# Where the fallback program lies in the instruction streams: behind each engine's first instructions, jumped over with a prefetch hint

## The chip, the cores and the metric

One core of one Trainium2 chip. Times are device microseconds of an execution. Runs carry a state, fast or slow; ratios use fast runs alone. The experiments ran on several chips, each beside `before` in the same rounds, and are compared with that. The profile is one execution; its span runs from the core's first to its last instruction and is about 1.8 us shorter than the time.

## The reference

Multi-head attention over one sequence of 2048 tokens, width 448, 16 heads of 28, in bf16:

```python
qkv = (x @ wqkv).reshape(B, S, 3, H, Dh).transpose(2, 0, 3, 1, 4)
q, k, v = qkv[0], qkv[1], qkv[2]
scores = einsum("bhqd,bhkd->bhqk", q, k) * Dh ** -0.5
o = einsum("bhqk,bhkd->bhqd", softmax(scores), v)
return o.transpose(0, 2, 1, 3).reshape(B, S, D) @ wo
```

## The kernel before

It holds two programs. The fast one (`F`) takes the softmax without its maximum and counts at the end whether every row sum lay in a safe range. The flag says yes for these inputs. If it said no, a slower general program (`R`) would run. Every engine gets both as one stream: fast program, flag, branch, general program, end.

```python
def body(e, eng):
    F.emit_engine(e, eng, fs)                     # the fast program, this engine's part
    eng.wait_ge(fs["dve"], F.flag_op.count)
    ok = eng.value_load(F.flag_ap)
    with eng.If(ok == 0):                         # not taken here: jumped over
        ...                                       # barrier
        R.emit_engine(e, eng, rs)                 # the general program
        ...
    if e == "sp":
        for gr in F.finish:                       # the output transfers have landed
            eng.wait_ge(gr.sem, 16 * gr.n)
```

As built, the general program has 6865 instructions on PE, 1161 on ACT, 595 on DVE, 107 on POOL and 45 on SP.

The fast program opens like this. ACT issues the loads of the first weights. SP issues four transposing loads of x, a quarter each. PE runs 14 groups of four matmuls on zeros: they start 0.40 to 0.43 us apart up to 4.55 us and 0.22 us apart from 4.84 us on, so that PE is in its short step when the first weights and the first quarter of x are there. Then PE projects K and Q of the first quarter, DVE copies K and ACT copies Q (`QT`) out of PSUM. PE then wants the second quarter of x, multiplies the first scores, and ACT begins its 362 exponentials, which are its bound to the end (87% of the chain that ended last).

## Time and profile before

| | before |
|---|---|
| time, median of fast runs | 355.51 us (355.34 to 355.72) |
| span of the profile | 353.3 us |
| weights and first quarter of x landed | 6.26 and 5.89 us |
| second quarter of x landed | 8.77 us |
| first exponential starts | 9.58 us |
| flag computed | 348.43 us |
| flag to end of the span | 4.90 us |

Read it as four stretches: an opening to 9.58 us, bound by loads (DMA share 0.99; PE's projections start 0.09 us after the weights have landed); 333 us of exponentials; 5.8 us of last products and copies up to the flag; and a close of 4.90 us after it, in which no engine computes. The lines behind it are in the prediction.

### The profile page before, as it was taken

Reading aid. Unit: us, or ns where it says so; the run is one execution under the profiler, and the core shown is the slowest. Engines: PE = TensorE matmul, PEld = TensorE weight load, DVE = VectorE, ACT = ScalarE, POOL = GpSimd, SP = SyncE. Lnnn points to the kernel's source line nnn. Section 1 sums busy time; section 2 is a strip of 40 time slices with the busy share of each in tenths; the row PEclk is TensorE's granted clock in tenths of the full one; section 3 lists DMA queues with packets and bytes.
Section 4 is the critical chain, followed back from the end, with each engine's and each line's share of the span. In section 5 each row is a group of like instructions: output and inputs, shape, how many; then the busy total and the mean of one; then the engine's idle time right before and its main releaser. Section 6 shows DMA issues by size and latency. Waiting matters only on the chain.

```text
span 353.3 us, 8533 instructions
## 1 busy us (share of the span) xinstructions
PE 332.5 (94%) x3601; PEld 97.5 (28%) x3601; DVE 328.9 (93%) x557; ACT 335.5 (95%) x367; POOL 68.4 (19%) x157
## 2 busy tenths in 40 slices
PE   7999999999999999999999999999999899999993
PEld 3333232223322222332322222223222222222231
DVE  1788999999999999999999999999999999999962
ACT  2999999999999999999999999999999999999971
POOL 7332030042043013104030121340120301010010
PEclk9999999999999999999999999999999999999999
DMA  9910010010100000010100101010000101020111
GB/s 186 216 24 2 15 39 2 5 32 2 32 19 18 0 5 32 0 34 3 33 2 4 33 1 33 3 33 2 13 21 5 32 30 58 16 71 13 42 34 59
DMA packets 21604, 10.63 MB, mean 30 GB/s; under 512 B 15676, under 2 KB 19516, under 8 KB 21560
## 3 DMA queue, kind: packets, MB, share of 16 engines
q1 hardware_dynamic: 20136, 9.71, 11.4%
q8 instruction: 30, 0.49, 0.6%
q10 hardware_dynamic: 1424, 0.31, 0.5%
q14 instruction: 14, 0.11, 0.1%
HBM read 5.83 MB, written 2.08 MB: 22 GB/s over the span
## 4 chain that ended last, share of the span: by engine, by line
ACT 87%; PE 7%; DVE 2%; DMA 2%; SPq 0%; issue 0%
ACT PT L935 87%; PE ps L846 3%; PE ps L894 2%; DMA xT<-in_x_dram 2%; DVE PD L961 1%; PE ps L758 1%; DVE PD L955 1%; DVE PD L963 1%; SPq L442 0%; PE ps L533 0%; PE ps L804 0%; PE ps L793 0%; PE ps L681 0%; PE ps L780 0%; DVE OUTS L810 0%
## 5 line engine op out<-in xcount | busy, mean ns | idle before, releaser
L935 ACT ACTIVATE PT<-ps 128x1024 bf16<-128x1024 f32 x362 | 332.4, 1252 | 1.3 <-PE ps L894 1.3
L955 DVE TENSOR_SCALAR PD<-ps 128x512 int16<-128x512 f32 x300 | 192.7, 682 | 7.8 <-PE ps L894 6.7
L894 PE MATMUL ps<-QT,KT 28*128 28x512 bf16 x1024 | 148.9, 384 | 11.1 <-ACT PT L935 9.5
L846 PE MATMUL ps<-PD,VC 128*32 128x512 f16 x900 | 80.0, 386 | 0.9 <-DVE PD L963 0.5
L894 PEld LDWEIGHTS ps<-QT,KT 28*128 28x128 bf16 x1024 | 37.9, 91 | 149.7 <-ACT PT L935 141.4
L846 PE MATMUL ps<-PT,V 128*32 128x512 bf16 x724 | 64.5, 385 | 0.7 <-DVE KT L517 0.2
L730 POOL TENSOR_TENSOR QT<-RB,OTS 128x128 bf16<-128x128 f32 x60 | 30.8, 544 | 161.7 <-DMA RB<-scr_r 161.5
L963 DVE TENSOR_SCALAR PD<-PD 128x2048 int16<-128x2048 int16 x75 | 53.5, 713 | 0.0
L961 DVE TENSOR_SCALAR PD<-PD 128x2048 int16<-128x2048 int16 x75 | 53.2, 709 | 0.1
L533 PE MATMUL ps<-xT,w_raw 128*32 128x512 bf16 x512 | 42.6, 385 | 1.4 <-DMA xT<-in_x_dram 0.6
L568 POOL TENSOR_SCALAR V<-VX 128x224 bf16<-128x224 f32 x32 | 12.6, 412 | 113.0 <-DVE VX L517 112.9
L846 PEld LDWEIGHTS ps<-PD,VC 128*32 128x32 bf16 x900 | 19.1, 94 | 32.6 <-issue 22.2
L846 PEld LDWEIGHTS ps<-PT,V 128*32 128x32 bf16 x724 | 15.7, 94 | 23.9 <-issue 20.7
L555 PE MATMUL ps<-w_raw,xT 128*128 128x112 bf16 x256 | 20.8, 215 | 0.0
L574 POOL TENSOR_SCALAR VC<-VX 128x112 bf16<-128x112 f32 (+1 forms) x48 | 19.0, 408 | 1.0
L555 PEld LDWEIGHTS ps<-w_raw,xT 128*128 128x128 bf16 x256 | 13.3, 98 | 10.9 <-issue 9.5
L533 PEld LDWEIGHTS ps<-xT,w_raw 128*32 128x32 bf16 x512 | 10.0, 94 | 19.5 <-issue 13.1
L681 PE MATMUL ps<-wop,QT 128*128 128x448 bf16 x48 | 13.5, 358 | 0.1
L517 DVE CAST KT<-ps 128x512 bf16<-128x512 f32 x16 | 11.0, 686 | 0.4 <-PE ps L533 0.3
L515 DVE TENSOR_SCALAR QT<-ps 128x512 bf16<-128x512 f32 x15 | 10.3, 685 | 0.3 <-PE ps L533 0.2
L713 DVE COPY OTS<-ps 128x512 f32<-128x512 f32 x15 | 10.3, 684 | 0.0
L517 DVE COPY VX<-ps 128x448 f32<-128x448 f32 x16 | 9.9, 618 | 0.3 <-PE ps L555 0.2
(50 smaller groups left out, 50.5 us busy)
## 6 DMA issues: line engine op xcount, KB each, us to landing
RB<-scr_r SPq DMA_DIRECT2D x60, 64.0 KB, 2.0
out_dram<-OUTS SPq DMA_DIRECT2D x16, 112.0 KB, 1.7
w_raw<-in_wqkv_dram SPq DMA_DIRECT2D x3, 249.0 KB, 4.3
wop<-in_wo_dram SPq DMA_DIRECT2D x16, 24.5 KB
w_raw<-in_wqkv_dram ACTq DMA_DIRECT2D x3, 87.0 KB, 3.9
scr_l<-OTS SPq DMA_DIRECT2D x15, 8.0 KB
LT<-scr_l SPq DMA_DIRECT2D x15, 8.0 KB, 1.6
scr_r<-RS SPq DMA_DIRECT2D x15, 8.0 KB, 1.4
```

The source lines that it names most:

```text
L517: fe = (lambda e: e.tensor_copy(evac[0](), evac[1](hold[0].banks[0])))
L533: ins = e.matmul(ps[32 * h:32 * h + 32, b * 512:(b + 1) * 512], w_raw[:, wi(c, it), col:col + 32], xT[:, it, c * 512:(c + 1) * 512], start ...
L555: ins = e.matmul(ps[:, b * 512 + j * GD:b * 512 + (j + 1) * GD], xT[:, it, n * 128:(n + 1) * 128], w_raw[:, wi(c, it), 2 * D + g * GD:2 * ...
L574: sc = P.add("pool", (lambda e, dst=dst, j=j: e.tensor_scalar(dst, src, TERM_C[j], 1.0, ALU.mult, ALU.mult)), deps=[ev, ms_c1[j]], after=[ ...
L681: return e.matmul(bank(hold[0].banks[0])[:, 0:D], QT[:, gg, n * 128:(n + 1) * 128], wop[:, gg, :], start=(gg == 0), stop=(gg == G - 1))
L730: nm = P.add("pool", (lambda e, k=k: e.tensor_tensor(QT[:, g, c * QCH + k * w_:c * QCH + (k + 1) * w_], RB[:, ub, k * w_:(k + 1) * w_], OT ...
L846: return e.matmul(ps[32 * h:32 * h + 32, accb(u) * 512:(accb(u) + 1) * 512], lhsT, rhs, start=first, stop=False, skip_group_check=True, ti ...
L894: return e.matmul(bank(b), KT[32 * h:32 * h + DH, g, kt * 128:(kt + 1) * 128], QT[32 * h:32 * h + DH, g, c * QCH:(c + 1) * QCH], start=Tru ...
L935: ex = P.add("act", (lambda e, p0=p0, w=w, b0=b0: e.activation(PT[:, p0 * 512:(p0 + w) * 512], bank(b0, w), AF.Exp, scale=ESCALE)), deps=[ ...
L955: r = P.add("dve", (lambda e, hold=hold, zs=zs, h=h: e.tensor_scalar(PD[:, zs, 0, h * 512:(h + 1) * 512], bank(hold[0].banks[0]), ZBIAS, 0 ...
L961: h1 = P.add("dve", (lambda e, zs=zs: e.tensor_scalar(PD[:, zs, 1, :], PD[:, zs, 0, :], float(TERM_D[1]), None, ALU.add)), deps=rs_ + [z_l ...
L963: h2 = P.add("dve", (lambda e, zs=zs: e.tensor_scalar(PD[:, zs, 2, :], PD[:, zs, 0, :], float(TERM_D[2]), None, ALU.add)), deps=rs_ + [z_l ...
```

## The change

Its intent is to take the far jump out of the close. The general program moves to a place behind the first few instructions of each engine. A jump there passes it by, and a prefetch hint (the engine's first instruction) is to have the target fetched by then. The main program falls through to its end.

```diff
+HEAD_OPS = {"sp": 3, "act": 6, "dve": 1, "pool": 13, "pe": 6}
 def body(e, eng):
-    F.emit_engine(e, eng, fs)
-    eng.wait_ge(fs["dve"], F.flag_op.count)
-    ok = eng.value_load(F.flag_ap)
-    with eng.If(ok == 0):
+    hint = eng.mark_branch_hint_location()
+    F.emit_engine(e, eng, fs, 0, lead, waited)          # lead = HEAD_OPS[e]
+    eng.br(go).branch_hint(hint)
+    with nc.body(slow, valid_engines=[eng.engine]):
         ...                                             # the general program, as it was
+        eng.br(end)
+    with nc.body(go, valid_engines=[eng.engine]):
+        F.emit_engine(e, eng, fs, lead, None, waited)
+        eng.wait_ge(fs["dve"], F.flag_op.count)
+        ok = eng.value_load(F.flag_ap)
+        eng.br_eq(ok, 0, on_true=slow, on_false=end)
+    nc.switch_bb(end)
```

## The prediction

> **What bounds the kernel now.** The change touches no arithmetic, so I first ask which part of the span could feel it. I read the page's busy line and chain, then the table of stretches, then the records of the closing instructions line by line, then the opening.

> ```profile
> PE 332.5 (94%) x3601; PEld 97.5 (28%) x3601; DVE 328.9 (93%) x557; ACT 335.5 (95%) x367; POOL 68.4 (19%) x157
> ACT PT L935 87%; PE ps L846 3%; PE ps L894 2%; DMA xT<-in_x_dram 2%; DVE PD L961 1%; PE ps L758 1%; DVE PD L955 1%; DVE PD L963 1%; SPq L442 0%; PE ps L533 0%; PE ps L804 0%; PE ps L793 0%; PE ps L681 0%; PE ps L780 0%; DVE OUTS L810 0%
> ```

> For 87% of the span the chain is ScalarE's exponentials. The diff leaves those instructions and their order alone, so the body should keep its length; only what comes before the first exponential and after the last output copy can move. The table of stretches (start:end, length, then busy time of PE, weight loads, DVE, ACT, POOL) sizes them:

> ```profile
> 0.00:9.60 9.60, 7.62 (x97) 2.95 (x97) 1.61 (x4) 2.10 (x4) 6.52 (x17) 1.00 0.99 194
> 9.60:342.70 333.10, 319.75 (x3452) 91.61 (x3451) 323.75 (x541) 332.35 (x362) 60.17 (x136) 1.00 0.10 25
> 348.40:353.40 5.00, 0.00 (x0) 0.00 (x0) 0.03 (x1) 0.00 (x0) 0.00 (x0) 0.95 0.27 88
> ```

> The last row is the find: for 5.0 us no engine computes, and the span still runs. What happens there is control flow: line 1652 loads the flag on each engine, line 1653 is the compare-and-branch over the general program, line 1665 is SP's wait for the output transfers, line 1635 the closing barrier (columns: duration in ns, start in us):

> ```profile
> L1652 ACTq TENSOR_LOAD <-FLAG x1: 493/493/493, 348.5 to 348.5; - x1
> L1652 SPq TENSOR_LOAD <-FLAG x1: 480/480/480, 349.1 to 349.1; - x1
> L1653 PEldq COMPARE_BRANCH  x1: 3344/3344/3344, 349.0 to 349.0; - x1
> L1653 DVEq COMPARE_BRANCH  x1: 72/72/72, 349.0 to 349.0; - x1
> L1635 POOLq DRAIN  x1: 112/112/112, 349.4 to 349.4; - x1
> L1635 SPq DRAIN  x1: 13/13/13, 350.8 to 350.8; - x1
> L1635 PEldq DRAIN  x1: 73/73/73, 352.4 to 352.4; - x1
> L1635 ACTq DRAIN  x1: 66/66/66, 352.8 to 352.8; - x1
> L1635 DVEq DRAIN  x1: 58/58/58, 353.0 to 353.0; - x1
> SPq L1635 <- PEq L1635: 2.5, 1, 2.5
> ```

> All five engines branch at about 349.0 (SP at 349.7). POOL is at the closing drain 0.4 us later, PE 3.3, ACT 3.8 and DVE 3.9 us later. The difference is the length of the general program that is jumped over: PE, ACT and DVE have 6865, 1161 and 595 instructions of it in the program as built, POOL 107 and SP 45. The trace's instruction packets agree: no such packet between 342 and 349.9 us except PE's, then five between 349.92 and 351.30 (four of 8192 bytes, one of 16384). SP stands at the barrier from 350.77 on and waits 2.5 us, as the last line says (it names PE; by the drain times the last to come is DVE). So the end of the span is set by instruction fetch after a taken branch, and SP, the only engine with real work left, is done 2.3 us before.

> [...] PE fetches one 16384-byte block per some 256 instructions all along with no stall seen, and the far branch costs 3.3 to 3.9 us, the near one 0.4. [...] the four records without a stall here are 45 to 72 ns. [...] here the groups of four warm-up matmuls start 0.427 us apart from 1.17 us on and 0.215 us apart from about 4.6 us on, 3.4 us later. [...]

> **The change, part by part.** (a) *End.* The general program now lies before the main one, so the untaken compare-and-branch falls into the closing block[...]. PE, ACT, DVE and POOL should reach the drain about 0.4 us after 349.0, as POOL does now. The barrier then waits for SP. Its path: last output transfer issued 348.627, landed 350.509, wait passed 350.553, drain ended 350.773. Now the last drain (DVE) ends at 353.100 and the span at 353.321, so the barrier takes 0.221. New end: 350.773 + 0.221 = 350.994. Gain: 353.321 - 350.994 = 2.33 us. The full 3.5 us of stall is not to be had, because the landing of the last output holds from 350.5 on.

> (b) *Hint at the front.* Each engine runs one more sequencer instruction before its first. I take 0.05 us, the size of an unstalled branch here. It is on the path: SP issues the first transpose at 0.73, ACT the first weight load at 0.73, and the first projection (6.35) starts when the weights' last part lands (6.26; x landed at 5.89). Cost 0.05 us.

> (c) *The jump at the front.* Measured from the end, hint to target ready is an estimate of 3.3 us on PE and 3.8 to 3.9 on ACT and DVE, so 4.1 and 4.6 us in the run. Engine by engine, from the opening's timeline (start, length, instruction):

> ```profile
> 1.16 4.92 PE L486 MATMUL ps<-ZM,ZW 128*32 128x512 bf16 x56 [1.16 <-POOL ZM L412]
> 5.09 0.20 ACT L416 ACTIVATE WARM<-WARM 128x1 f32<-128x1 f32 x1
> 7.12 0.23 DVE L458 TENSOR_SCALAR id_f<-iota_i 128x128 f32<-128x128 int32 x1 [5.58 <-POOL iota_i L456]
> 8.30 0.60 ACT L513 ACTIVATE QT<-ps 128x512 bf16<-128x512 f32 x1 [3.01 <-PE ps L533]
> ```

> DVE jumps at about 1.5 and next has work at 7.12; ACT jumps after its warm-up at 5.3 and works again at 8.30; POOL's 13 operations reach to 7.1; SP jumps after 8.18. All four are covered. PE is the tight one: its six operations are 24 of the 56 warm-up matmuls and run until 3.71 in cold steps, so it idles perhaps 0.4 us, until 4.1. The 32 remaining need one cold step and seven warm ones: 4.1 + 0.43 + 7 x 0.215 = 6.04, still before the weights at 6.26. [...]

> (d) *Fetch traffic at the front.* Five to ten packets of 8 or 16 KB now run where DMA is 99% busy. A PE packet at 11.5 us took 0.94 us beside such traffic, so the engine that carries one falls behind by up to that[...]. x has 0.37 us of room, the weights none. The early start of the fetch (data packets begin at 1.82) helps. I book 0.2 us.

> Sum: -2.33 + 0.05 + 0 + 0.2 = -2.1 us; 355.48 - 2.1 = 353.4. I round up to 353.5, as each unknown at the front can only cost.

> **Rivals.** *The hint does not act, or late.* Then PE stalls at its jump from about 2 to 5.4-6 us, with 1.7 us or more without matmuls; the clock could stay cold, 32 matmuls at 0.107 us take 3.4 instead of 1.9 us, the first projection starts 0.8 to 2.5 us late, and ACT, jumping at 5.1, could be 0.5 us late too. Time 354.2 to 355.9: the gain is paid back. Against it: a hint exists for this purpose, and PE keeps queued matmuls to run. For it: no trace here has one, and DMA is full.
> *Another wait takes the end.* The outputs land at 350.5 whatever the engines do; that is in the sum. If the closing block also lies across a block boundary that was not fetched, some engine stalls again by up to 3.3 us and nothing is gained; the steady sequential fetch over 350 us speaks against it.
> *The time outside the span moves.* The profiled run took 355.11 with a span of 353.32, so 1.8 us lie outside. Further instruction packets at 353.14 to 354.12 show fetching after the end too; with another place in its block this part could shrink or grow by an estimated 0.5 us.
> *A second activation table load in the new block.* The existing one took 1.28 us; ACT is idle from 5.29 to 8.30, so it would be hidden.

> **Range and chances.** The end's gain is nearly certain in size; the front takes back between 0.05 and about 1.3 us, and the part outside the span gives or takes 0.5. Range 352.8 to 354.7. A 2% change is 7.1 us, more than the whole dead end: chance of faster by over 2% 0.01, within 2% 0.985, slower by over 2% 0.005.

> **What would show it.** Right: in the new profile all compare-and-branches of the flag are short, every drain but SP's begins near 349, SP's comes last and the span ends 0.2 us after it; the wait of SP at the barrier vanishes; instruction packets appear between 1 and 4 us. Step (c) is wrong if the warm-up matmuls have a gap much over 0.5 us or are still 0.427 us apart after 5 us. Step (d) is wrong if the weights land outside 6.3 to 6.6 us. The prediction fails if the first exponential, at 9.58 now, starts after 10.8, or if an engine other than SP still reaches the last drain after 351.

Its sum came to -2.33 + 0.05 + 0 + 0.2 = -2.1 us. The 0 is the term of (c): it rested on an assumption about the gap in PE's warm-up. That the closing block would be at hand in (a) was an estimate from POOL's 0.4 us, and the 0.2 us of (d) one from the single packet of 0.94 us. The block fetch is measured: PE has 28 packets of 16384 bytes before the close, with 196 to 276 recorded PE and weight-load instructions (254 on average) from one to the next. These are the "regular block fetches" below.

## The result, and the profile after

The median is 357.41 us against 355.51, but one of its four runs, 364.10 us, is slow. The four fast runs of the changed kernel (356.89 to 357.83, median 357.0, mean 357.2) are 1.5 us slower by the medians and 1.7 by the means, and their median lies 2.3 us above the upper end of the predicted range. A ratio here is the mean time of one kernel's fast runs over that of the other's in the same rounds, so not quite the ratio of the medians; it is 1.0047 (95% interval 1.0029 to 1.0064).

The profiled execution fell in the slow state: 362.3 us, with PE's granted clock at 0.50 from 11.86 to 35.75 us. The four fast runs have spans of 355.1 to 356.0. I use this profile for the opening and for the close. The very end of the opening, from 11.86 us to the first exponential, lies in that stretch: from the first score product to the exponential it takes 0.65 us instead of 0.43. A second profile of the same kernel (run `again`) has its half clock from 13.20 us only, takes 0.43 us there, and gives the same front.

The close first: the stretch after the flag, the branches on the flag (line 1674) and the drains at the closing barrier (line 1638), columns as in the prediction.

```profile
359.50:362.30 2.80, 0.00 (x0) 0.00 (x0) 0.00 (x0) 0.00 (x0) 0.00 (x0) 1.00 0.38 128
```

```profile
L1674 PEldq COMPARE_BRANCH  x1: 82/82/82, 360.1 to 360.1; - x1
...
L1638 ACTq DRAIN  x1: 8/8/8, 360.1 to 360.1; - x1
L1638 PEldq DRAIN  x1: 8/8/8, 360.2 to 360.2; - x1
L1638 DVEq DRAIN  x1: 17/17/17, 360.2 to 360.2; - x1
...
L1638 SPq DRAIN  x1: 13/13/13, 362.1 to 362.1; - x1
```

PE's branch takes 82 ns instead of 3344, all drains but SP's come within 0.2 us of the branches, and SP's is last. Flag to end is 2.84 us instead of 4.90. The close does what was predicted of it.

The opening gives it back almost twice over. First the jump over the general program (line 1658) on the two engines that matter, then the timeline of the opening (start, length, engine, line, operation; in brackets the idle time before it and what ended it):

```profile
L1658 PEldq COMPARE_BRANCH  x1: 3164/3164/3164, 1.3 to 1.3; - x1
...
L1658 ACTq COMPARE_BRANCH  x1: 56/56/56, 4.8 to 4.8; - x1
```

```profile
4.57 2.12 PE L486 MATMUL ps<-ZM,ZW 128*32 128x512 bf16 x32 [0.57 <-issue]
...
7.91 1.91 PE L533 MATMUL ps<-xT,w_raw 128*32 128x512 bf16 x32 [1.23 <-issue]
...
11.94 0.62 PE L533 MATMUL ps<-xT,w_raw 128*32 128x512 bf16 x4 [2.11 <-DMA xT<-in_x_dram]
12.14 0.60 ACT L513 ACTIVATE QT<-ps 128x512 bf16<-128x512 f32 x1 [5.92 <-issue]
...
13.45 1.02 ACT L935 ACTIVATE PT<-ps 128x1024 bf16<-128x1024 f32 x1 [0.70 <-PE ps L894]
```

The same places in the timeline of before (ACT's copy at 8.30 us is in the prediction):

```profile
6.35 1.91 PE L533 MATMUL ps<-xT,w_raw 128*32 128x512 bf16 x32 [0.26 <-issue]
...
8.82 0.40 PE L533 MATMUL ps<-xT,w_raw 128*32 128x512 bf16 x4 [0.56 <-DMA xT<-in_x_dram]
...
9.58 22.11 ACT L935 ACTIVATE PT<-ps 128x1024 bf16<-128x1024 f32 x24 [0.68 <-PE ps L894]
```

The reader should see three delays. The first projection starts at 7.91 instead of 6.35 us: the weights land at 7.82 instead of 6.26. The second quarter of x is used at 11.94 instead of 8.82. And ACT's copy starts at 12.14 instead of 8.30, after 5.92 us of "issue", that is, waiting for nothing that the profile shows, although PE had finished Q at 9.82. ACT's copy is the last to come: the first score product waits for it until 12.80. The first exponential is 3.87 us late (3.75 in the second profile, without the half clock). 2.06 us gained at the end and 3.87 lost at the front make a loss of 1.8; the means of the fast runs differ by 1.7.

Why the loads are late shows in the DMA view of 8 to 10 us: the window cut into 40 slices of 0.05 us, with what the DMA engines moved in each (a packet counts where it starts). Before:

```profile
GB/s 266 241 220 159 67 102 169 276 297 287 292 292 287 292 292 287 287 307 276 297 276 302 282 297 287 297 282 292 287 297 297 276 292 186 52 82 87 102 102 82
```

After:

```profile
GB/s 251 292 251 287 276 261 256 26 20 0 0 0 0 0 0 0 0 0 5 5 10 5 10 5 10 10 5 15 5 15 5 10 10 10 15 189 282 297 281 288
```

For 28 slices, 1.4 us, nearly nothing moves while the loads are in full swing. The trace has one PE instruction packet of 16384 bytes at 7.88 to 8.96 us, and load packets that take 18 ns elsewhere last up to 1444 ns. (Single packets are read from the packed trace; no view prints them.) The hole begins about 0.5 us after the packet's start and lasts 0.8 us beyond its end. There are shorter holes at 3.0 to 4.0 us (after PE's first packet, 1.88 to 3.08) and at 6.9 to 7.7 and 10.8 to 11.2 us (after 8192-byte packets). The kernel before has such a hole as well, beside PE's regular block fetch at 11.48 us, where it hurt nothing: the exponentials ran on without a gap.

Counted in slices of 0.05 us, this holds over all 15 traces. After every 16384-byte packet of the first 13.5 us there are 0.8 to 1.6 us in which load packets start at under a fifth of their usual rate. In the seven traces without a jump at the front, no such stop longer than 0.3 us occurs between 2.3 and 11.4 us.

### The profile page after: what moved, and what is told of

It is laid out like the page before. It is cut to its first block, busy times and chain, and to the rows that moved or that the text cites. A ratio compares the mean times of both kernels' runs of the same rounds, so it can differ in the third digit from the quotient of the medians.

```text
span 362.3 us, 8545 instructions
## 1 busy us (share of the span) xinstructions
PE 340.0 (94%) x3601; PEld 98.6 (27%) x3601; DVE 329.3 (91%) x557; ACT 337.0 (93%) x367; POOL 66.9 (18%) x157
## 3 DMA queue, kind: packets, MB, share of 16 engines
q1 hardware_dynamic: 20136, 9.71, 12.1%
## 4 chain that ended last, share of the span: by engine, by line
ACT 82%; PE 14%; DMA 2%; issue 1%; DVE 0%; SPq 0%
ACT PT L935 82%; PE ps L894 5%; PE ps L846 4%; PE ps L533 2%; PE ps L555 2%; DMA xT<-in_x_dram 2%; PE ps L758 1%; PE ps L804 0%; PE ps L793 0%; PE ps L681 0%; PE ps L780 0%; DVE OUTS L810 0%; ACT QT L513 0%; SPq L1656 0%; DVE FLAG L992 0%
## 5 line engine op out<-in xcount | busy, mean ns | idle before, releaser
L935 ACT ACTIVATE PT<-ps 128x1024 bf16<-128x1024 f32 x362 | 333.9, 1283 | 7.0 <-PE ps L894 6.9
L955 DVE TENSOR_SCALAR PD<-ps 128x512 int16<-128x512 f32 x300 | 192.7, 680 | 14.0 <-PE ps L894 12.6
L894 PE MATMUL ps<-QT,KT 28*128 28x512 bf16 x1024 | 150.7, 395 | 12.5 <-ACT PT L935 10.5
L846 PE MATMUL ps<-PD,VC 128*32 128x512 f16 x900 | 80.5, 389 | 0.4 <-DVE PD L955 0.2
L894 PEld LDWEIGHTS ps<-QT,KT 28*128 28x128 bf16 x1024 | 37.5, 91 | 153.8 <-ACT PT L935 140.3
L846 PE MATMUL ps<-PT,V 128*32 128x512 bf16 x724 | 65.2, 389 | 0.5 <-DVE KT L517 0.2
L961 DVE TENSOR_SCALAR PD<-PD 128x2048 int16<-128x2048 int16 x75 | 53.1, 709 | 0.1
L963 DVE TENSOR_SCALAR PD<-PD 128x2048 int16<-128x2048 int16 x75 | 52.3, 698 | 0.0
L533 PE MATMUL ps<-xT,w_raw 128*32 128x512 bf16 x512 | 45.3, 407 | 3.4 <-DMA xT<-in_x_dram 2.1
L846 PEld LDWEIGHTS ps<-PD,VC 128*32 128x32 bf16 x900 | 19.2, 94 | 31.9 <-issue 23.4
L555 PE MATMUL ps<-w_raw,xT 128*128 128x112 bf16 x256 | 22.9, 230 | 0.0
L846 PEld LDWEIGHTS ps<-PT,V 128*32 128x32 bf16 x724 | 15.9, 95 | 24.0 <-issue 21.0
L574 POOL TENSOR_SCALAR VC<-VX 128x112 bf16<-128x112 f32 (+1 forms) x48 | 18.2, 392 | 1.0
L555 PEld LDWEIGHTS ps<-w_raw,xT 128*128 128x128 bf16 x256 | 14.8, 105 | 12.9 <-issue 11.8
L533 PEld LDWEIGHTS ps<-xT,w_raw 128*32 128x32 bf16 x512 | 10.2, 96 | 22.7 <-issue 16.5
L681 PE MATMUL ps<-wop,QT 128*128 128x448 bf16 x48 | 13.5, 358 | 0.2 <-DVE PD L955 0.2
L515 DVE TENSOR_SCALAR QT<-ps 128x512 bf16<-128x512 f32 x15 | 10.2, 683 | 0.1
L713 DVE COPY OTS<-ps 128x512 f32<-128x512 f32 x15 | 10.2, 681 | 0.0
```

Of the source, the lines that this page charges most:

```text
L533: ins = e.matmul(ps[32 * h:32 * h + 32, b * 512:(b + 1) * 512], w_raw[:, wi(c, it), col:col + 32], xT[:, it, c * 512:(c + 1) * 512], start ...
L555: ins = e.matmul(ps[:, b * 512 + j * GD:b * 512 + (j + 1) * GD], xT[:, it, n * 128:(n + 1) * 128], w_raw[:, wi(c, it), 2 * D + g * GD:2 * ...
L574: sc = P.add("pool", (lambda e, dst=dst, j=j: e.tensor_scalar(dst, src, TERM_C[j], 1.0, ALU.mult, ALU.mult)), deps=[ev, ms_c1[j]], after=[ ...
L681: return e.matmul(bank(hold[0].banks[0])[:, 0:D], QT[:, gg, n * 128:(n + 1) * 128], wop[:, gg, :], start=(gg == 0), stop=(gg == G - 1))
L846: return e.matmul(ps[32 * h:32 * h + 32, accb(u) * 512:(accb(u) + 1) * 512], lhsT, rhs, start=first, stop=False, skip_group_check=True, ti ...
L894: return e.matmul(bank(b), KT[32 * h:32 * h + DH, g, kt * 128:(kt + 1) * 128], QT[32 * h:32 * h + DH, g, c * QCH:(c + 1) * QCH], start=Tru ...
```

## The experiments

Two theories for the front: **D**, the fetch packets hold up the loads; **A**, ACT's jump stalls by itself. A third, **T**, says the half clock of the profiled run is the loss. For the later runs there are rules on when a hint is served, that is, when its target is fetched ahead: **R**, only by the engine's next regular block fetch; **L**, given enough time. "Front of before" below means no jump at the front.

| run | what jumps at the front | weights landed | second x quarter landed | ACT's QT copy | first exponential | flag to end | ratio to before (95%) |
|---|---|---|---|---|---|---|---|
| before | none | 6.26 | 8.77 | 8.30 | 9.58 | 4.90 | |
| changed kernel | all five | 7.82 | 11.89 | 12.14 | 13.45 | 2.84 | 1.0047 (1.0029 to 1.0064) |
| again | all five | 7.94 | 11.99 | 12.25 | 13.33 | 2.77 | 1.0022 (1.0001 to 1.0043) |
| no_hint | all five | 8.06 | 13.23 | 11.80 | 14.04 | 2.85 | 1.0111 (1.0047 to 1.0176) |
| act_kept | all but ACT | 7.77 | 11.34 | 9.82 | 12.15 | 3.43 | 1.0014 (0.9993 to 1.0034) |
| pe_kept | all but PE | 6.43 | 10.32 | 10.53 | 11.62 | 4.55 | 1.0089 (1.0033 to 1.0146) |
| pe_act_kept | DVE, POOL, SP | 7.08 | 9.91 | 9.13 | 10.72 | 4.63 | 1.0023 (1.0009 to 1.0038) |
| pe_only | PE | 7.76 | 11.15 | 9.81 | 11.96 | 4.09 | 1.0018 (0.9999 to 1.0038) |
| act_only | ACT | 6.01 | 8.97 | 9.22 | 10.30 | 4.87 | 1.0009 (0.9989 to 1.0029) |
| late_jump | none; all near 55 us | 6.21 | 9.12 | 8.98 | 10.06 | 3.04 | 1.0132 (1.0104 to 1.0160) |
| fetch_only | none | 6.27 | 9.22 | 8.53 | 10.03 | 4.85 | 0.9991 (0.9976 to 1.0005) |
| end_hint | none | 6.32 | 9.06 | 8.37 | 9.87 | 4.60 | 0.9970 (0.9955 to 0.9984) |
| act_hint_early | none | 6.46 | 8.89 | 8.51 | 9.70 | 2.49 | 0.9930 (0.9917 to 0.9943) |
| act_tail_jump | none; ACT before its last two copies | 6.24 | 8.78 | 8.29 | 9.59 | 2.49 | 0.9923 (0.9911 to 0.9936) |
| hints_after_boundary | none | 6.52 | 9.13 | 8.57 | 9.94 | 4.96 | 0.9988 (0.9971 to 1.0004) |

The columns in microseconds come from one profile each; kernels that share the front of before differ by up to 0.5 us in the first exponential, so a difference of that size is no effect. Part of this spread is seen: with the same stream PE's warm-up goes over to its short step near 3.9 us in `end_hint` but not before 6.7 in `late_jump`, whose first projection then starts at 7.03 us, with the weights there at 6.21. The profiles of the changed kernel and of `again` are slow, all others fast.

**again.** No edit.

> The changed kernel unchanged, for a profile in the fast state. Theory F (instruction fetch traffic at the front delays the loads, and PE and ACT stall at their jumps): the first exponential starts near 13.4 us (9.58 before) in the fast state too, the span is near 355.2 us, the time 357.0. Rival T (the loss is the throttled clock seen in the first profile, 23.9 us at half rate): in the fast state the first exponential is back near 9.7 us. If F, the fast time of 357.0 is -2.05 us at the end plus about 3.9 us at the front.

The profile fell in the slow state again, so a full profile of the fast state is still missing. But its half clock begins at 13.20 us, and up to there the opening is the same as in the first profile, with the first exponential at 13.33:

```profile
13.33 1.94 ACT L935 ACTIVATE PT<-ps 128x1024 bf16<-128x1024 f32 x2 [0.48 <-PE ps L894]
```

Its fast runs are also slower than before (median of all 356.65 against 355.58). T is out for the fast runs: their clock is 0.998 to 1.000 and they lose all the same, though on this chip only about 0.8 us, where 3.75 lost and 2.13 gained would make 1.6. The other 0.8 us is not explained.

**act_kept, pe_kept.** One engine keeps the old layout; the other four jump.

```diff
+KEEP = ("act",)          # pe_kept: ("pe",)
 def body(e, eng):
+    if e in KEEP:
+        F.emit_engine(e, eng, fs)
+        eng.wait_ge(fs["dve"], F.flag_op.count)
+        ok = eng.value_load(F.flag_ap)
+        with eng.If(ok == 0):
+            ...                                # barrier, general program
+        return
```

> ACT alone keeps its general program behind the main one, so ACT has no jump at the front; the other four jump. Theory A (ACT's jump, which its hint does not serve, is what holds the first exponential): first exponential near 9.7 to 10.5 us. Theory D (PE's two 16 KB instruction packets hold up the loads: weights 7.8 instead of 6.3 us, second quarter of x 11.9 instead of 8.8 us): weights and x stay late, PE waits for x until 11.9, first exponential near 12.5 to 13 us. At the end ACT takes the far branch again, so the closing is as long as before (about 4.9 us after the flag): time about 355.6 by A, about 358.5 by D.

> PE alone keeps its general program behind the main one, so no 16 KB packets at the front and no gap in the warm-up; the others jump. Theory D: weights land near 6.4 us and the second quarter of x near 8.9 us again. If D is the whole cause, first exponential near 9.7 us. If ACT's jump also stalls on its own, ACT's first copy (QT) still starts near 12.1 us and the first exponential near 12.8 us. End: PE takes the far branch, closing about 4.2 us after the flag. Time about 355.0 by D alone, about 358 if ACT stalls by itself.

Without ACT's jump, ACT copies Q at 9.82, at once when PE is done:

```profile
9.82 0.60 ACT L513 ACTIVATE QT<-ps 128x512 bf16<-128x512 f32 x1 [3.48 <-PE ps L533]
11.38 0.40 PE L533 MATMUL ps<-xT,w_raw 128*32 128x512 bf16 x4 [1.61 <-DMA xT<-in_x_dram]
```

That takes off 1.2 to 1.3 of some 3.8 us: x still lands at 11.34 and the first exponential starts at 12.15, nearer D's 12.5 than A's 9.7 to 10.5. A alone is out. (D's time, 358.5, was missed: the run took 356.17, and its close 3.43 us instead of the 4.9 forecast.) Without PE's jump the weights are back at 6.43, as D expects, but x lands at 10.32, not 8.9: with PE's jump gone, those of the other four still hold it. ACT is then the last to come (10.53). So neither engine alone carries the loss. `pe_kept` has one run of 361.15 us counted as fast at a clock of 0.981, which widens its interval.

**no_hint.** The changed kernel without hints.

```diff
-    hint = eng.mark_branch_hint_location()
-    eng.br(go).branch_hint(hint)
+    eng.br(go)
```

> The changed kernel without the five prefetch hints. If the hints act, PE's packet comes some 0.5 us later (jump at 1.3 instead of hint at 0.85), and PE resumes near 5.0 instead of 4.5 us; ACT the same as with the hint if its hint never acted (its packets came 1.07 us after its jump), else later by some us. Rival: the hints themselves do harm (they fetch too early, beside the loads): the first exponential is then earlier than 13.4 us. Time 357.0 to 358 if the hints act on PE alone.

PE resumes at 5.98 us instead of 4.51, and its packet starts at 3.37 instead of 1.88. PE's hint therefore acts and saves about 1.5 us of PE's stall, where 0.5 was expected; the hints are not the harm. Here PE's own stall does count: its warm-up stays in long steps to the end, and the first projection starts at 9.42 us although the weights landed at 8.06. The last to come is again x, at 13.23. One of four runs (362.35, clock 0.974) widens the interval.

**pe_act_kept, pe_only, act_only.** The same edit with other engines in `KEEP`: each part of the jump by itself.

> PE and ACT keep the general program behind the main one; DVE, POOL and SP jump at the front. Theory D: only DVE's 8 KB packets remain at the front, second quarter of x near 9.2 to 9.6 us, first exponential near 10 to 10.4 us; the end is set by ACT's far branch, about as long as before. Time 355.8 to 356.3. Rival (the packets don't add up, ACT's jump alone did it): first exponential near 9.7, time 355.3.

> PE alone jumps at the front, the other four keep the layout of before. Isolates PE's 16 KB packets. Theory D: two packets near 1.9 to 3.1 and 7 to 8 us, loads held beside each: weights near 7.3, second quarter of x near 10.5 to 11, first exponential near 11 to 11.6 us. Rival (the packets do little, PE's stall and cold clock are what delays): weights near 6.3, second quarter of x near 9, first exponential near 9.9. The end is as long as before (ACT, DVE branch far): time about 357 by D, 355.7 by the rival.

> ACT alone jumps at the front, the others keep the layout of before. Isolates ACT's jump. If ACT's resume is held by the same crowd of loads: packets near 5 to 6 and 7.5 to 9 us, ACT's first copy (QT) at 9 to 10.5 instead of 8.3, second quarter of x 0.5 to 1 us late, first exponential near 10.3 to 11. If ACT resumes 3.9 us after its jump: QT copy at about 8.4 and first exponential at 9.7 to 10.2. End: PE and DVE branch far, flag to end 4.6 to 4.9. Time about 356 to 356.5, or 355.6.

`pe_act_kept`: the three engines bring three 8192-byte packets (2.16, 5.80 and 7.67 us), the last two followed by a stop of 0.55 and 0.75 us in the loads. x and the first exponential are each about 0.3 us later than D's range, so ACT's jump alone did not do it.

PE alone, which issues no load at all, moves the loads by 1.5 and 2.4 us. The timeline of this run:

```profile
7.85 1.91 PE L533 MATMUL ps<-xT,w_raw 128*32 128x512 bf16 x32 [1.09 <-DMA xT<-in_x_dram]
...
11.20 0.40 PE L533 MATMUL ps<-xT,w_raw 128*32 128x512 bf16 x4 [1.43 <-DMA xT<-in_x_dram]
```

Here PE's warm-up ends at 6.76 us and PE waits 1.09 us for data, so it is the loads and not PE's gap or its clock that set the start. The rival is out: PE's jump makes the loads late. That it does so through its two packets (1.88 and 8.03 us) rests on timing: the loads stop after each for 1.25 and 1.5 us and nowhere else in this opening. (The tool names x as releaser of the first wait; by the landings the weights, at 7.76, are the last.)

ACT alone shows the other half. The view is its timeline:

```profile
9.02 0.40 PE L533 MATMUL ps<-xT,w_raw 128*32 128x512 bf16 x4 [0.90 <-DMA xT<-in_x_dram]
9.22 0.60 ACT L513 ACTIVATE QT<-ps 128x512 bf16<-128x512 f32 x1 [3.73 <-issue]
```

ACT jumps at 4.11 us. Its only packet at the front starts at 7.41, 3.3 us later. Away from the opening's loads the packets of a far branch start 0.8 to 1.2 us after it: 0.9 to 1.1 at the end of before, where the last outputs still go out until 350.1 us, and 0.8 to 1.2 in `late_jump`, where no data packet starts from 52 to 58 us. The packet ends at 7.82 and ACT works 1.40 us later, 1.1 us after PE had finished Q. So the crowd held the fetch. That ACT's fetch holds the crowd this run does not show: x landed at 8.97, within the spread of the runs without a jump (8.77 to 9.22), where 0.5 to 1 us of delay was expected. In the changed kernel ACT jumps at 4.85 and works at 12.14, and a packet ends 1.49 us before that, at 10.65; that this one is ACT's is inferred from that distance, as the queue is shared and a packet carries no engine's name.

The delays of the first exponential roughly add up: PE 2.38, ACT 0.72, the other three 1.14, together 4.24, against 3.75 to 3.87 for all five. With a spread of 0.5 us in each, no more can be said.

**late_jump.** Hint near 45 us, jump near 55 us, where DMA is idle (a share of 0.03 from 50 to 55.8 us, 0.00 from there to 57.8).

```diff
-    hint = eng.mark_branch_hint_location()
-    F.emit_engine(e, eng, fs, 0, lead, waited)
+    F.emit_engine(e, eng, fs, 0, ahead, waited)      # operations before 45 us of the schedule
+    hint = eng.mark_branch_hint_location()
+    F.emit_engine(e, eng, fs, ahead, lead, waited)   # before 55 us
```

> The changed kernel with hint and jump moved out of the opening: hint near 45 us, jump near 55 us of the schedule, where the DMA engines are nearly idle. Theory D (fetch packets hold up the opening's loads): weights land near 6.3, the second quarter of x near 8.8, first exponential near 9.6 us as before; the end keeps its 2.0 us. Time 353.4 to 354.0 if the hints serve PE and ACT in the middle. Rival A (a jump costs its engine some us whatever the place): a gap of 3 to 5 us in ACT's or PE's work near 55 us, time 356 or more.

The front is that of before, as D says, and the close is short, yet the time is 5 us worse. PE's and ACT's timelines at the jump:

```profile
57.77 2.86 ACT L935 ACTIVATE PT<-ps 128x1024 bf16<-128x1024 f32 x3 [1.98 <-issue]
```

```profile
57.57 0.39 PE L894 MATMUL ps<-QT,KT 28*128 28x512 bf16 x2 [1.71 <-issue]
```

PE's hint ran at 44.85, but its packet came only at 54.98, 0.25 us before the jump, and PE stalled for 2.29 us; ACT jumped at 54.45 and had nothing. After this idle time PE ran at half clock from 58.13 to 68.37 us (granted clock 0.54 on average from 57.8 to 69). DVE went through its jump without a gap. Rival A is right here: a jump in the middle costs its engine.

**fetch_only.** No jump at the front; PE's first instruction is a hint for its closing branch.

```diff
+    hint = eng.mark_branch_hint_location() if e == "pe" else None
     F.emit_engine(e, eng, fs)
...
-    with eng.If(ok == 0):
+    jump = eng.br_ne(ok, 0, on_true=end, on_false=slow)
+    if hint is not None:
+        jump.branch_hint(hint)
```

> The layout of before, no jump at the front; PE alone gets a prefetch hint as its first instruction, for its closing branch, so that one 16 KB instruction packet runs at about 1.9 to 3.1 us and nothing else changes. Theory D: load packets stall beside it, weights land 0.4 to 1.0 us late, the second quarter of x near 9.6 to 10 us (8.77 before), first exponential near 10.3 to 10.8 us. Rival: a packet delays only the engine that carries it and little is seen: second quarter of x within 0.3 us of 8.8, first exponential near 9.7. Time 356.2 to 356.8 by D, 355.6 by the rival.

A miss that taught more than a hit. No packet ran at the front, so it says nothing on D. But PE's closing branch, 349 us after the hint, took 0.39 us instead of 3.3: the target was there:

```profile
L1659 PEldq COMPARE_BRANCH  x1: 391/391/391, 349.5 to 349.5; - x1
```

PE had no more packets before the close than in before (28 in both), so a regular block fetch seems to have brought something else because of the hint; what it brought, the trace does not say.

**end_hint.** All five closing branches hinted near the end.

```diff
+HINT_OPS = {"sp": 4, "act": 2, "dve": 14, "pool": 4, "pe": 20}
+    lead = len(F.order[e]) - HINT_OPS[e]
+    F.emit_engine(e, eng, fs, 0, lead, waited)
+    hint = eng.mark_branch_hint_location()
+    F.emit_engine(e, eng, fs, lead, None, waited)
...
+    eng.br_ne(ok, 0, on_true=end, on_false=slow).branch_hint(hint)
```

> The layout of before, nothing at the front; each engine gets a prefetch hint for its closing branch some 5 us ahead of it (PE 20 operations, DVE 14, ACT 2, SP and POOL 4 before their last). If the hint serves: instruction packets near 341 to 344 us, all drains but SP's near 349, the span 2.3 us shorter than before with the front unchanged: time 353.2 to 353.6. If the hint doesn't serve ACT (as its jump at the front suggests): ACT's drain 3.8 us after its branch, time within 0.3 us of before.

PE and DVE are served, ACT is not. Its drains:

```profile
L1638 PEldq DRAIN  x1: 62/62/62, 350.2 to 350.2; - x1
L1638 DVEq DRAIN  x1: 52/52/52, 350.3 to 350.3; - x1
...
L1638 ACTq DRAIN  x1: 67/67/67, 353.4 to 353.4; - x1
```

So the close still waits for ACT, and the gain is 0.3%.

**act_hint_early, act_tail_jump.** Two ways to help ACT: its hint 100 operations before its end; or no hint, and instead a jump over the general program between its last exponential and its last two copies.

```diff
-HINT_OPS = {"sp": 4, "act": 2, ...}
+HINT_OPS = {"sp": 4, "act": 100, ...}                # act_hint_early
```

```diff
+if e == "act":                                       # act_tail_jump
+    F.emit_engine(e, eng, fs, 0, len(F.order[e]) - 2, waited)
+    eng.br(go)
+    ...                                              # general program; then go: the last two copies, flag, end
```

> end_hint with ACT's hint 100 operations before its end (about 90 us) instead of 2. If ACT's hint was unserved because it came after the last block boundary that ACT crosses before its end: now it is served, ACT's drain comes near the flag's 1.3 us, flag to end about 2.7 us, time about 353.3. If ACT's hints are never served, as at the front and near 45 us: ACT's drain again 3.7 us after its branch, time as end_hint, about 354.3.

> Candidate. PE and DVE as in end_hint (closing branch hinted some 5 us ahead). ACT instead jumps over its general program between its last exponential and its two last copies, where it stands idle for 4.1 us anyway, and then falls through to the end. Theory (a far jump costs ACT about 3.3 us after the jump, and hides in that idle time): ACT's last two copies keep their distance to the last exponential (4.07 us in before), ACT's drain comes with the others, SP's drain is last, flag to end about 2.6 to 2.8 us instead of 4.9, front as before: time 2.0 us under the before of the same rounds, about 353.3. Rival: the jump takes longer than the idle time and pushes the copies: gain under 1.5 us.

Both do it. Drains of `act_hint_early`:

```profile
L1638 ACTq DRAIN  x1: 93/93/93, 349.6 to 349.6; - x1
...
L1638 DVEq DRAIN  x1: 52/52/52, 349.8 to 349.8; - x1
...
L1638 SPq DRAIN  x1: 13/13/13, 350.8 to 350.8; - x1
```

And ACT's first copy after the far jump of `act_tail_jump`, in its timeline:

```profile
346.86 0.54 ACT L807 ACTIVATE OUTS<-ps 128x448 bf16<-128x448 f32 x1 [4.07 <-PE ps L804]
```

The jump (341.49 us) was over by 344.14, when ACT's sequencer ran its next instruction, and hid in the 4.07 us that ACT waits there for PE in before too. Medians are 353.03 (`act_tail_jump`) and 353.16 us against 355.77 of before: 2.7 and 2.6 us faster, better than both kernels of this study. This is the 2.3 us that was predicted for the close and a little more, without a touch to the front.

**hints_after_boundary.** `act_hint_early` with ACT's hint 55, DVE's and PE's 4 operations before the end: on the near side of each engine's last regular block fetch (ACT near 279, DVE near 341, PE near 342 us).

> act_hint_early with the hints moved to the near side of each engine's last regular block fetch: ACT 55 operations before its end (about 50 us, its last regular fetch is near 278 us), DVE 4 (last fetch near 340.6), PE 4 (near 342.1). Rule R (a hint is served by the next regular block fetch and by nothing else): all three unserved, drains of PE, ACT and DVE 3 to 4 us after the branch as in before, flag to end 4.7 to 5.0 us, time as before (355.8). Rival L (lead time is what counts, and ACT's 2-operation lead of 8 us was too short for it): ACT served with its 50 us lead; DVE and PE, with 2 to 3 us, partly. Rival P (PE fetches a hinted block at once, as at the front of the changed kernel): PE's packet within 1.1 us of its hint and its branch short, ACT and DVE not.

```profile
L1638 ACTq DRAIN  x1: 67/67/67, 352.9 to 352.9; - x1
L1638 PEldq DRAIN  x1: 64/64/64, 353.0 to 353.0; - x1
L1638 DVEq DRAIN  x1: 58/58/58, 353.5 to 353.5; - x1
```

All three unserved (branch to drain 3.5 to 4.1 us, against 0.4 to 0.6 for PE and DVE in `end_hint` and for ACT in `act_hint_early`), ACT with 56 us of lead (hint at 293.1, branch at 349.4). Rule R fits what was measured at the close, and for ACT lead time is not what counts. For PE and DVE the lead was short as well (2.6 and 3.3 us instead of 8.6 and 11.0 in `end_hint`), so there the two are not told apart. PE's hint at 346.8 brought no packet before the branch either, so "PE fetches at once" is out there.

## Why the prediction was wrong

- **Bound and target: right.** The body kept its length: the exponentials lasted 333.03 us in before and 333.06 in `no_hint`, whose profile is fast. The close was instruction fetch after a far branch, ended by PE, ACT and DVE (3.3, 3.8 and 3.9 us from branch to drain).
- **Step (a), the end: right in mechanism, near in size.** Predicted gain 2.33 us, measured 2.06 (2.13 in `again`): SP's last output transfer was issued 0.41 us after the flag instead of 0.20. In all seven runs in which SP jumps early it is 0.40 to 0.52 us, in the other eight 0.20 or 0.21; why is not shown. `act_hint_early`, with 2.49 us from flag to end, shows 2.4 us to be had.
- **Step (b), the hint itself: 0.05 predicted, about 0.1 measured** (SP's first issue at 0.84 instead of 0.73, ACT's at 0.82).
- **Step (d), the fetch traffic, failed**, and is most of the error. It booked 0.2 us, from the picture that a packet delays only the DMA engine that carries it. The runs show nearly all load traffic standing still during or just after a packet, 1.4 us for a PE packet of the changed kernel, and several such holes: 1.56 us on the weights and 3.12 on the second quarter of x; PE's jump alone gives 1.50 and 2.38. With ACT's jump taken out (`act_kept`), 2.57 of the 3.87 us remain. The warning was in the trace of before: after the PE packet at 11.48 us load packets took up to 1558 ns, and hardly one started for a microsecond. I had quoted that packet's own 0.94 us and not looked at what ran beside it.
- **Step (c), the jumps, failed on ACT.** It called ACT covered because 3.8 us from the hint ends long before 8.30. ACT's hint was not served (in `act_only` no packet comes until 3.3 us after the jump), and the fetch came late beside the loads: 7.3 us from jump to work, not 3.8. On PE it was roughly right: by the prediction's own count of steps the warm-up gap is 0.8 us instead of 0.4, and the loads were later than PE in any case. The jumps also came earlier than it said (DVE 0.9, PE 1.3 and ACT 4.8 us instead of about 1.5, 2 and 5.3): PE's branch began at 1.34 us while its queued matmuls ran on to 3.99. The estimate from the close holds only away from such a burst (ACT in `late_jump` 3.3 us, in `act_tail_jump` 2.7). Nor is the 3.4 us that the prediction read for the rise of PE's clock steady: in `end_hint` and `late_jump`, with PE's stream unbroken, it is 2.7 and over 5.5.
- **The rival "hint does not act, or late"** named ACT and a full DMA, and put the time at up to 355.9. It was the right direction, thought too unlikely, and it too left the held loads out. Its picture of PE came true in `no_hint` alone.

Still open: by what mechanism all load packets stand still, and why this outlasts the instruction packet; why PE's hint at the very front was served at once (packet 1.03 us after it and 0.54 after the jump's start; without the hint it came 2.10 after the jump) while PE's hint in `late_jump` got its packet 10.1 us later and the one in `hints_after_boundary` none before the branch; which 8192-byte packet belongs to which engine; why the profiled executions of the changed kernel, twice, fell into the half clock, which other runs of it avoid.
